# One written order for the spectrum products of a long-convolution kernel, and two weight loads on another queue

## The chip, the core and the metric

The kernel runs on one core of a Trainium2 chip. The time is device microseconds of one execution; the number given is the median of several runs. The core's engines are TensorE (PE), VectorE (DVE), ScalarE (ACT) and GpSimd (POOL); SyncE (SP), ScalarE and GpSimd issue DMAs. Each engine takes its instructions strictly in the order in which they stand in its program, and waits on semaphores for the others.

## What is computed

The reference runs two kinds of layer twice, forward, and then the gradients of all inputs. Layer A is a short convolution of `k` over four steps, a product with `v`, a convolution over the whole sequence by Fourier transform, and a gate; layer B is a dense network with SiLU.

```python
def _A_ref(q, k, v, shift_k, ssm_k, ssm_D):        # S = 2048, D = 448
    k_shift = sum(k_pad[:, t:t + S, :] * shift_k[:, ks - 1 - t] for t in range(ks))
    kv = k_shift * v
    y = irfft(rfft(kv padded to 2 S) * rfft(ssm_k padded to 2 S))[:S] + kv * ssm_D
    return q * y
x = A_q
x = x + _A_ref(_layernorm(x), A_k, A_v, ...); x = x + _B_ref(_layernorm(x), B_w1, B_w2)
x = x + _A_ref(_layernorm(x), A_k, A_v, ...); x = x + _B_ref(_layernorm(x), B_w1, B_w2)
```

`kv` and its convolution with `ssm_k` do not depend on `x`. They are made once, at the start, and used in both A layers.

## The kernel before

The function `_ssm_prefix` makes that convolution in the first 90 us or so. `Main` follows with both layers forward and backward, and `_ssm_suffix` with the gradients of the convolution. The change lies in the second half of `_ssm_prefix`, from `for i in range(4, 7)` (L499) to L560.

The transform has two stages. Stage 1 (`stage1_kv`, L465) writes the tile `A1kv`, and the same for the filter writes `KAB`. What follows works on 14 pieces of 1024 columns (numbered ci, 0 to 13), two of which make one block of 2048 (g, 0 to 6). For every piece or block there are these steps:

- **P and p** (`spec_k`, L468 to L475): the filter's stage 2. Two matmuls of 512 columns into a PSUM tile (`_fft_stage2_full`, L244), and a copy back to `KAB` by ScalarE (L116) or VectorE (L117). Pieces 0 to 7 are done between the convolutions; 8 to 13 in the loop at L499.
- **Q** (L474 and L282): GpSimd issues one store of two pieces to DRAM (`spec_K`) and four DMAs that write the other half of `KAB` with swapped partitions.
- **Z and z** (L511 to L516, the transposes at L514): 16 transposes of 128x128 of `A1kv` into one PSUM tile, and a copy to `ZkvA` or `ZkvB`. Block 3 lies across both and is copied in two halves.
- **F and f** (L244, and L523 or L116/L117): stage 2 of `kv`, two matmuls, and a copy back to `ZkvA` or `ZkvB`. After some pieces GpSimd issues a store to DRAM (`spec_KV`, L540).
- **M** (L542): VectorE multiplies piece ci with both halves of `KAB` into a tile `pab`, of which there are four.
- **V and v** (L253, L254): the inverse step, 16 matmuls from `pab` into PSUM, and a copy to `A1kv`, whose old contents are no longer needed.

All PSUM tiles of these steps share four slots of two banks (tag "A"). In the source the steps stand in loops: all p, then all Z, then for each ci F, f, M and, two pieces late, V. The order in which each engine then gets them is made by the compiler's scheduler, which ranks by place in the source and by an estimate of times, and so is the choice of PSUM slots. Which engine copies is chosen by `_Bal`, which adds up estimated times of ScalarE and VectorE and takes the lesser (L92 to L111).

The weights `w1` and `w2` of layer B are loaded in the same stretch. ScalarE issues the DMAs, behind its copies of pieces 4 and 7 (L523 to L534). First reader of `w1sb` is `Hh` (L638, L642), of `w2sb` it is `O` (L798).

After the stage come, on TensorE in a fixed order, the transposes of `grad_out` (L615) and `ys` (L563), which reads all of `A1kv`; ScalarE copies its results into `Ysb` (L564). VectorE makes the gate of the first chunk (L684, L685), which writes `X`, and its norm (L301 to L309), whose result is transposed (L626) for the first matmuls with `w1`. Four tile slots are used twice: `Ysb` lies where `ZkvA` was (tag W2), `X` where `ZkvB` was (WX), `w1sb` where `kT` was (W1), `w2sb` where `v_n` was (WB). A tile's first write waits until everything that read the earlier one is done, stores included.

Of the kernel before, what the change touches and what calls it, by code (L numbers as in the profile page):

```python
# [11 lines left out]
BF16 = mybir.dt.bfloat16  # L12
ACT = mybir.ActivationFunctionType
ALU = mybir.AluOpType
# [3 lines left out]
P = 128  # L18
S = 2048
D = 448  # L20
F = 1792
# [10 lines left out]
NCI = SPEC // 1024  # L32
# [81 lines left out]
def _copy(nc, eng, out, in_):  # L114
    if eng is nc.scalar:
        return nc.scalar.copy(out, in_)  # L116
    return eng.tensor_copy(out, in_)  # L117


KPARTS = [(0, 128), (128, 256), (256, 384), (384, 448)]  # L120


class K:
# [12 lines left out]
def kernel(  # L136
# [58 lines left out]
    k.mdp = ctx.enter_context(tc.tile_pool(name="mdp", bufs=1, reuse_waits="tile"))  # L195
    k.wtp = ctx.enter_context(tc.tile_pool(name="wtp", bufs=1, reuse_waits="tile"))
    ys = _ssm_prefix(k)
    k.psum = ctx.enter_context(tc.tile_pool(name="psum", bufs=1, space=PSUM, reuse_waits="tile"))
    k.bal.reset()
# [40 lines left out]
def _fft_stage2_full(k, Zf, ci, psum):  # L240
    ps = psum.tile([P, 1024], FP32, name="ps_s2", **k.pt["s2"])
    for hh in range(2):
        o = slice(hh * 512, hh * 512 + 512)
        k.nc.tensor.matmul(ps[:, o], lhsT=k.Gpre[:, G_FWDF, :] if ci % 2 else k.Gsb[:, G_FWD, :], rhs=Zf[:, o], start=True, stop=True)  # L244
    return ps


def _fft_inv_stage2_full(k, pa, pb, B1, ci, psum):
    nc = k.nc
    ga, gb = (G_IAF, G_IBF) if ci % 2 else (G_IA, G_IB)  # L250
    pv = psum.tile([P, 8, P], FP32, name="ps_v", **k.pt["v"])
    for i in range(8):
        nc.tensor.matmul(pv[:, i, :], lhsT=pa[:, i * P:(i + 1) * P], rhs=k.Gpre[:, ga, :], start=True, stop=False)  # L253
        nc.tensor.matmul(pv[:, i, :], lhsT=pb[:, i * P:(i + 1) * P], rhs=k.Gpre[:, gb, :], start=False, stop=True)  # L254
    _copy(nc, k.bal.pick(1024), B1[:, 8 * ci:8 * ci + 8, :].rearrange("p a b -> p (a b)"), pv[:].rearrange("p a b -> p (a b)"))


def _fft_inv_stage2_half(k, pa, pb, B1, ci, psum, cnd):
# [21 lines left out]
def _swap_halves_dma(k, dst, src, lo, hi):  # L280
    for o, i in SWAPS:
        k.nc.gpsimd.dma_start(out=dst[o, lo:hi], in_=src[i, lo:hi])  # L282


def _pm(ap2d):
    return ap2d.rearrange("(p j) d -> p j d", j=J)
# [47 lines left out]
def _ssm_prefix(k):  # L334
    nc, tc = k.nc, k.tc
    bal = k.bal
    k_pm = _pm(k.A_k[0])
    v_pm = _pm(k.A_v[0])
    with ExitStack() as es:
        spec = es.enter_context(tc.tile_pool(name="spec", bufs=1))  # L340
        work = es.enter_context(tc.tile_pool(name="pwork", bufs=2))
        psum = es.enter_context(tc.tile_pool(name="ppsum", bufs=3, space=PSUM))

        a_ = dict(tag="A", bufs=4)
# [4 lines left out]
        KAB = spec.tile([P, 2, SPEC], BF16, name="KAB")  # L349
        A1K = KAB[:, 0, :].rearrange("p (a c n s) -> p a c n s", c=2, n=16, s=2)  # L350
        A1Kf = KAB[:, 0, :].rearrange("p (a b) -> p a b", b=P)
        Ka = KAB[:, 1, :]
        Z = Ka.rearrange("p (a b) -> p a b", b=P)
# [15 lines left out]
        for h in range(2):  # L369
            for lo, hi in KPARTS[2 * h:2 * h + 2]:  # L370
                nc.sync.dma_start(out=ksb[lo // P][:hi - lo], in_=k.A_ssm_k[lo:hi, :])
# [14 lines left out]
        def k_turn(lo, hi):  # L386
            n = hi - lo
            kview = ksb[lo // P][:n].rearrange("p (n1 n2) -> p n2 n1", n2=16)
            pt = psum.tile([P, 2, 1024], BF16, name="ps_kt", **a_)
            pv = pt[:, :, 0:8 * n].rearrange("p g (i d) -> p g i d", d=n)  # L390
            for i in range(16):
                nc.tensor.transpose(pv[:, i // 8, i % 8, :], kview[:, i, :], k.ident[:n, :n])
            for g in range(2):
                _copy(nc, bal.pick(8 * n, dve_ns=0.53), Kt[:, 8 * g:8 * g + 8, lo:hi], pv[:, g])
# [12 lines left out]
        for lo, hi in ((0, 256), (256, D)):  # L407
            for plo, phi in KPARTS[lo // P:lo // P + 2]:
                k_turn(plo, phi)
# [17 lines left out]
        for jq in range(4):  # L427
            pt = psum.tile([DC, ND, 4, P], BF16, name="ps_kT", **a_)
# [40 lines left out]
        def spec_k(cp):  # L469
            for ci in (2 * cp, 2 * cp + 1):  # L470
                o = Ka[:, ci * 1024:(ci + 1) * 1024]
                _copy(nc, bal.pick(1024), o, _fft_stage2_full(k, o, ci, psum)[:])
            lo, hi = cp * 2048, (cp + 1) * 2048
            nc.gpsimd.dma_start(out=k.SPEC_d["K"][:, lo:hi], in_=Ka[:, lo:hi])  # L474
            _swap_halves_dma(k, KAB[:, 0, :], Ka, lo, hi)  # L475
# [20 lines left out]
        Zkv = [k.wk.tile([P, H2], BF16, name="ZkvA", tag="W2"), k.wk.tile([P, H2], BF16, name="ZkvB", tag="WX")]  # L496
        k.gb0 = _hd(k, [P, 4, D], "gb0")
        nc.sync.dma_start(out=k.gb0[:], in_=_pm(k.grad_out[0])[:, 0:4, :])
        for i in range(4, 7):  # L499
            spec_k(i)  # L500

        B1 = A1kv[:].rearrange("p b c n s -> p (b c n s)").rearrange("p (a x) -> p a x", x=P)

        def zkv(lo, hi):
            h = lo // H2
            return Zkv[h][:, lo - h * H2:hi - h * H2]

        def zdst(g):
            cuts = [(0, 16)] if g != 3 else [(0, 8), (8, 16)]
            return [(lo, hi, zkv(2048 * g + lo * P, 2048 * g + hi * P).rearrange("p (a b) -> p a b", b=P)) for lo, hi in cuts]  # L510
        for g in range(7):  # L511
            pt = psum.tile([P, 16, P], BF16, name="ps_tr", **a_)
            for i in range(16):
                nc.tensor.transpose(pt[:, i, :], B1[:, 16 * g + i, :], k.ident[:])  # L514
            for lo, hi, o in zdst(g):
                _copy(nc, bal.pick((hi - lo) * P, dve_ns=0.53), o, pt[:, lo:hi, :])  # L516
        hold = []

        def cons_prod(ci, ps):
            sl = slice(ci * 1024, (ci + 1) * 1024)  # L520
            xs = zkv(ci * 1024, (ci + 1) * 1024)
            if ci in (4, 7):
                with tc.issue_after(nc.scalar.copy(xs, ps[:]).ins):  # L523
                    if ci == 4:
                        w1x = k.wk.tile([P, ND * F + 2 * D], BF16, name="w1sb", tag="W1")
                        k.w1sb = w1x[:, 0:ND * F].rearrange("p (c f) -> p c f", f=F)
                        k.xq = [w1x[:, ND * F:].rearrange("p (j d) -> p j d", d=D)]
                        nc.scalar.dma_start(out=k.w1sb[:, 0:3, :], in_=k.B_w1[0:384, :].rearrange("(c p) f -> p c f", p=P))
                        nc.scalar.dma_start(out=k.w1sb[:, 3, :], in_=k.B_w1[320:448, :])
                    else:  # L530
                        w2x = k.wk.tile([P, (NF + 2) * D], BF16, name="w2sb", tag="WB")
                        k.w2sb = w2x[:, 0:NF * D].rearrange("p (c d) -> p c d", d=D)
                        k.xq.append(w2x[:, NF * D:].rearrange("p (j d) -> p j d", d=D))
                        nc.scalar.dma_start(out=k.w2sb, in_=k.B_w2.rearrange("(c p) d -> p c d", p=P))  # L534
                bal.add("act", 1.4)
            else:
                _copy(nc, bal.pick(1024), xs, ps[:])
            if ci in (1, 3, 5, 6, 8, 10, 12, 13):
                lo = (ci - (ci not in (6, 13))) * 1024
                nc.gpsimd.dma_start(out=k.SPEC_d["KV"][:, lo:(ci + 1) * 1024], in_=zkv(lo, (ci + 1) * 1024))  # L540
            pab = work.tile([P, 2, 1024], BF16, name="pab", tag="pab", bufs=4)
            nc.vector.tensor_tensor(out=pab[:], in0=xs.rearrange("p (o f) -> p o f", o=1).broadcast_to((P, 2, 1024)), in1=KAB[:, :, sl], op=ALU.mult)  # L542
            bal.add("dve", 1.25)
            hold.append((pab[:, 1], pab[:, 0], ci))
            if len(hold) > 2:
                pa, pb, cj = hold.pop(0)
                _fft_inv_stage2_full(k, pa, pb, B1, cj, psum)

        for ci in range(NCI):
            cons_prod(ci, _fft_stage2_full(k, zkv(ci * 1024, (ci + 1) * 1024), ci, psum))  # L550
        for pa, pb, cj in hold:
            _fft_inv_stage2_full(k, pa, pb, B1, cj, psum)

        B1v = B1.rearrange("p a (c n s) -> p a c n s", c=2, n=16)
        k.Ysb = k.wk.tile([P, J, D], BF16, name="Ysb", tag="W2")
# [819 lines left out]
```

## Time and profile before

| | us |
|---|---|
| median of 3 runs | 702.48 (701.94 to 702.93) |
| the profiled execution | 701.8 |
| its span in the profile | 700.0 |

The profile's page gives busy times of the engines over the span, a picture in 40 slices, the chain of work that ended last, groups of instructions by source line, and DMA issues. Other answers of the trace give the same for a window, in order of time (timeline), or as sums of who waited for whom. In a timeline a row is: start, duration, engine, line, operation, written tile, read tiles, shapes, count; in square brackets the idle time of that engine before it and what ended it. PE is TensorE, DVE VectorE, ACT ScalarE, POOL GpSimd. A duration is longer than the distance from one start to the next, since instructions of one engine overlap a little.

### The profile page before, as it was taken

Reading aid. Unit: us, or ns where it says so; the run is one execution under the profiler, and the core shown is the slowest. Engines: PE = TensorE matmul, PEld = TensorE weight load, DVE = VectorE, ACT = ScalarE, POOL = GpSimd, SP = SyncE. Lnnn points to the kernel's source line nnn. Section 1 sums busy time; section 2 is a strip of 40 time slices with the busy share of each in tenths; the row PEclk is TensorE's granted clock in tenths of the full one; section 3 lists DMA queues with packets and bytes.
Section 4 is the critical chain, followed back from the end, with each engine's and each line's share of the span. In section 5 each row is a group of like instructions: output and inputs, shape, how many; then the busy total and the mean of one; then the engine's idle time right before and its main releaser. Section 6 shows DMA issues by size and latency. Waiting matters only on the chain.

```text
span 700.0 us, 14553 instructions
## 1 busy us (share of the span) xinstructions
PE 666.0 (95%) x5897; PEld 358.8 (51%) x5933; DVE 484.1 (69%) x1131; ACT 432.9 (62%) x522; POOL 101.3 (14%) x173
## 2 busy tenths in 40 slices
PE   6898789999999999999999999999999999999996
PEld 5876545454444444434444444544554555555664
DVE  6688862676889948899578874853946545538991
ACT  5888766968856857769577585223554553554431
POOL 1057110110011100111000100010111211102311
PEclk9999999999999999999999999999999999999999
DMA  8999938459899976698677799959557888966981
GB/s 321 270 298 306 376 84 210 118 107 243 219 231 249 246 200 166 146 240 221 185 165 194 194 242 329 262 172 229 177 208 280 307 279 307 352 188 215 331 293 42
DMA packets 199798, 161.03 MB, mean 230 GB/s; under 512 B 147698, under 2 KB 180213, under 8 KB 198963
## 3 DMA queue, kind: packets, MB, share of 16 engines
q1 hardware_dynamic: 184550, 111.78, 58.8%
q0 software_dynamic: 10368, 36.29, 15.3%
q10 hardware_dynamic: 4812, 12.04, 5.0%
q8 instruction: 46, 0.75, 0.4%
q14 instruction: 22, 0.17, 0.1%
HBM read 66.05 MB, written 54.60 MB: 172 GB/s over the span
## 4 chain that ended last, share of the span: by engine, by line
PE 57%; DVE 22%; issue 10%; ACT 5%; POOL 3%; DMA 2%; POOLq 0%; DVEq 0%; ACTq 0%
PE ps_d L1046 19%; PE ps_n L836 8%; PE ps_h L638 6%; PE ps_g L638 6%; PE ps_o L798 5%; DVE ln_st L301 2%; DVE lb_v L994 2%; PE ps_v L265 2%; PE ps_cv L449 2%; POOL rstd L306 2%; DVE n L309 1%; DVE lb_v L997 1%; DVE lb_v L998 1%; DVE X L802 1%; PE ps_h L642 1%
## 5 line engine op out<-in xcount | busy, mean ns | idle before, releaser
L1046 PEld LDWEIGHTS <-dstat 128*128 128x128 bf16 x896 | 84.0, 98 | 77.8 <-issue 4.0
L836 PE MATMUL ps_n<-w1T,ghT 128*128 128x448 bf16 x448 | 96.6, 353 | 2.0 <-DVE ghT L821 1.7
L798 PE MATMUL ps_o<-w2sb,aT 128*128 128x448 bf16 x448 | 89.2, 353 | 0.7 <-DVE X L802 0.7
L638 PE MATMUL ps_h<-nT,w1sb 128*128 128x512 bf16 (+1 forms) x410 | 83.5, 336 | 2.2 <-ACT Dall L116 1.0
L116 ACT CAST ghT<-ps_g 128x1024 bf16<-128x1024 f32 (+1 forms) x54 | 48.4, 899 | 58.4 <-PE ps_g L642 47.7
L638 PE MATMUL ps_g<-nT,w2T 128*128 128x512 bf16 x317 | 77.9, 379 | 2.2 <-DVE Dall L117 0.5
L836 PEld LDWEIGHTS <-ghT 128*128 128x128 bf16 x448 | 41.4, 98 | 50.7 <-DVE ghT L821 6.7
L798 PEld LDWEIGHTS <-aT 128*128 128x128 bf16 x448 | 43.2, 98 | 41.1 <-issue 2.8
L638 PEld LDWEIGHTS <-w1sb 128*128 128x128 bf16 x420 | 39.2, 98 | 36.7 <-issue 7.2
L781 ACT ACTIVATE aT<-ps_h 128x1024 bf16<-128x1024 f32 (+1 forms) x48 | 44.2, 921 | 19.4 <-PE ps_h L638 10.5
L116 ACT CAST Dall<-ps_h 128x1024 bf16<-128x1024 f32 (+2 forms) x60 | 54.3, 904 | 0.0
L994 DVE SCALAR_TENSOR_TENSOR lb_v<-lb_u,n 128x448 bf16<-128x448 bf16 x60 | 37.2, 620 | 24.6 <-ACT lb_u L840 24.1
L791 ACT ACTIVATE Dall<-Dall 128x1024 bf16<-128x1024 bf16 (+1 forms) x48 | 53.2, 1186 | 0.1
L638 PEld LDWEIGHTS <-w2T 128*128 128x128 bf16 x336 | 31.3, 98 | 42.1 <-issue 7.2
L306 POOL TENSOR_TENSOR rstd<-ln_ve,mhalf 128x2 f32<-128x2 f32 (+1 forms) x24 | 19.9, 831 | 221.1 <-DVE ln_ve L305 221.1
L1046 PE MATMUL ps_d<-X,dstat 128*128 128x448 bf16 x224 | 47.9, 353 | 0.0
L1046 PE MATMUL ps_d<-go,dstat 128*128 128x448 bf16 x224 | 47.2, 353 | 0.0
L1046 PE MATMUL ps_d<-n3m,dstat 128*128 128x448 bf16 x224 | 46.4, 353 | 0.0
L1046 PE MATMUL ps_d<-n1m,dstat 128*128 128x448 bf16 x224 | 46.3, 353 | 0.0
L840 ACT ACTIVATE lb_u<-ps_n,rstd 128x448 bf16<-128x448 f32 x32 | 20.5, 640 | 28.7 <-PE ps_n L836 24.3
L116 ACT CAST A1g<-ps_v 128x1024 bf16<-128x1024 f32 x14 | 14.9, 1066 | 36.5 <-PE ps_v L265 36.5
L802 DVE TENSOR_TENSOR X<-X,ps_o 128x448 bf16<-128x448 bf16 x32 | 19.5, 610 | 21.3 <-PE ps_o L798 21.1
(206 smaller groups left out, 1111.6 us busy)
## 6 DMA issues: line engine op xcount, KB each, us to landing
dstat<-a_d SPq DMA_DIRECT2D x28, 512.0 KB, 5.0
dstat<-g_d SPq DMA_DIRECT2D x28, 512.0 KB, 5.2
a_d<-turned SPq DMA_DIRECT2D x16, 512.0 KB, 3.0
g_d<-turned SPq DMA_DIRECT2D x16, 512.0 KB, 3.2
a_d<-turned SPq DMA_DIRECT2D x16, 384.0 KB, 2.7
g_d<-turned SPq DMA_DIRECT2D x16, 384.0 KB, 3.0
spec_K<-KAB POOLq DMA_DIRECT2D x7, 512.0 KB, 5.4
KAB<-KAB POOLq DMA_DIRECT2D x28, 128.0 KB, 4.6
```

What stands on the lines that cost most here:

```text
L116: return nc.scalar.copy(out, in_)
L265: nc.tensor.matmul(pv[:, r ^ (ci & 1), i, :], lhsT=src[ri, i * P:(i + 1) * P], rhs=k.Gsb[ri, g, ri], start=first, stop=not first)
L306: nc.gpsimd.tensor_tensor(out=r[:, lo:hi], in0=ve[:, lo:hi], in1=k.mhalf[:, lo:hi], op=ALU.pow)
L638: self.nc.tensor.matmul(ps, lhsT=w[:, b, ft * P:(ft + 1) * P], rhs=x[:, b], start=(start and b == 0), stop=(stop and b == bs[2]))
L781: self.last_silu = nc.scalar.activation(aT[hh][:, o:o + hi - lo, :], ps(lo, hi), ACT.Silu)
L791: self.nc.scalar.activation(dT[hh][:, o:o + n, :], dT[hh][:, o:o + n, :], ACT.Derivative_silu)
L798: nc.tensor.matmul(po[:, :D], lhsT=aT[ft // 7][:, ft % 7, tl * P:(tl + 1) * P], rhs=self.w2sb[:, ft, :], start=(ft == 0), stop=(ft == NF - 1))
L802: self.last_o = nc.vector.tensor_tensor(out=X[:, t, :], in0=X[:, t, :], in1=po[:, :D], op=ALU.add)
L836: nc.tensor.matmul(pn[:, :D], lhsT=gh[ft // 7][:, ft % 7, tl * P:(tl + 1) * P], rhs=self.w1T[:, ft, :], start=(ft == 0), stop=(ft == NF - 1))
L840: nc.scalar.activation(u0[:], pn[:, :D], ACT.Identity, scale=k.rstd[2 * L + 1][:, t:t + 1], accum_out=cp[:, tl, 0:1])
L994: nc.vector.scalar_tensor_tensor(out=v[:], in0=u0, scalar=-1.0 / D, in1=n_t, op0=ALU.mult, op1=ALU.mult, accum_out=cp[:, 1:2])
L1046: self.nc.tensor.matmul(ps[:, :D], lhsT=st[:, t, :], rhs=mov[:, t, :], start=(first and t == 0), stop=(last and t == NT - 1))
```

## The change

The steps of the stage from P8 on are written as one list of tokens. A capital is work on TensorE (P, Z, F, V), on VectorE (M) or the DMAs of a Q; a small letter is the copy out of PSUM, with its engine as the last letter, `a` for ScalarE and `d` for VectorE (`z3y` and `z3x` are the two halves of block 3). The list is traced in a `manual_schedule` of TensorE, ScalarE, VectorE and GpSimd: each of these engines gets its instructions of the list in the list's order.

```diff
+PRODUCTS = """
+P9 P10 P11 P12 p9a p10d p11a P13 p12d P8 p8a Z0 Q5 p13d Z1 z0d Z2 z1a Q6 F0 z2d F1 f0a F2 f1d F3 f2a F4 Q4 M0 F5 f3a Z4
+f4a Z6 z4d f5a z6d F8 f8a F9 M1 F12 F13 f9a Z5 M2 f12a V0 z5d f13a Z3 v0a F11 z3yd z3xd F7 f11a M3 F6 f7a F10 V1 M4 f6a
+V2 f10a M6 V3 v1a M5 V4 v2a M11 V5 v3a V6 M10 v4a V11 M12 v5a V10 M13 v6a V12 v11a M7 V13 v10a M8 V7 v12a M9 V8 v13a v8d
+V9 v7a v9a
+"""
...
-        for i in range(4, 7):
-            spec_k(i)
...
-                _copy(nc, bal.pick((hi - lo) * P, dve_ns=0.53), o, pt[:, lo:hi, :])
...
-                        nc.scalar.dma_start(out=k.w1sb[:, 0:3, :], in_=k.B_w1[0:384, :].rearrange("(c p) f -> p c f", p=P))
-                        nc.scalar.dma_start(out=k.w1sb[:, 3, :], in_=k.B_w1[320:448, :])
...
+            seen.add(ci)
+            for lo, hi in ((0, 2), (2, 4), (4, 6), (6, 7), (7, 9), (9, 11), (11, 13), (13, 14)):
+                if ci in range(lo, hi) and seen >= set(range(lo, hi)):
+                    nc.gpsimd.dma_start(out=k.SPEC_d["KV"][:, lo * 1024:hi * 1024], in_=zkv(lo * 1024, hi * 1024))
+                    if lo == 6:
...
+                        nc.gpsimd.dma_start(out=k.w1sb[:, 0:3, :], in_=k.B_w1[0:384, :].rearrange("(c p) f -> p c f", p=P))
+                        nc.gpsimd.dma_start(out=k.w1sb[:, 3, :], in_=k.B_w1[320:448, :])
+                    elif lo == 9:
...
+                        nc.gpsimd.dma_start(out=k.w2sb, in_=k.B_w2.rearrange("(c p) d -> p c d", p=P))
...
+        do = dict(P=P_, p=p, Q=Q, Z=Z_, z=z, F=F_, f=f, M=M, V=V, v=v)
+        with tc.manual_schedule(engines={e.engine for e in (nc.tensor, nc.scalar, nc.vector, nc.gpsimd)}):
+            for tok in PRODUCTS.split():
+                args = [int("".join(x for x in tok if x.isdigit()))]
+                if tok[-1] in "ad":
+                    args += [int(tok[-2] == "y"), nc.scalar if tok[-1] == "a" else nc.vector]
+                do[tok[0]](*args)
```

The stores of `spec_KV` keep their eight ranges of pieces; each is issued when its last piece has been copied, so their order follows the list: (0,1), (2,3), (4,5), (13), (11,12), (7,8), (6), (9,10). The loads of `w1` come right behind the store of piece 6 and that of `w2` right behind the store of pieces 9 and 10, all on GpSimd's queue. The matmuls, products and copies are the same in number and shape as before.

## The prediction

> **What bounds the kernel now.** I read the page first. TensorE fills 95% of the span, and the chain that ended last is TensorE work for 57% of it, so the kernel is one long dependent chain. A stage that ends earlier moves everything behind it, unless a transfer stops that. The change touches one stage only, from the last convolution work to `ps_y`, 52.5 to 90.7 us. So I asked for busy times in that stretch (columns: length, PE, weight loads, VectorE, ScalarE, GpSimd, clock, DMA share, GB/s).
>
> ```profile
> PE 666.0 (95%) x5897; PEld 358.8 (51%) x5933; DVE 484.1 (69%) x1131; ACT 432.9 (62%) x522; POOL 101.3 (14%) x173
> ...
> 52.50:90.70 38.20, 29.59 (x405) 22.70 (x407) 32.48 (x30) 29.59 (x30) 15.96 (x32) 1.00 0.96 329
> ```
>
> No engine is full: in 38.2 us TensorE has 29.6, VectorE 32.5, ScalarE 29.6. The DMA engines are full (0.96). So the stage is bound either by the order of the work on in-order engines, or by transfers. The waits of 52 to 91 us tell which (engine, tile and line, what it waited for: us in total, times, longest):
>
> ```profile
> PE ps_v L253 <- DVE pab L542: 7.4, 7, 2.4
> ACT A1kv L116 <- PE ps_v L254: 4.5, 4, 2.4
> DVE ZkvB L117 <- PE ps_s L244: 1.8, 1, 1.8
> DVE A1kv L117 <- PE ps_v L254: 1.3, 2, 1.2
> ```
>
> All are engines waiting for each other, none for a transfer. The timelines show one such wait:
>
> ```profile
> 77.37 2.35 DVE L542 TENSOR_TENSOR pab<-ZkvB,KAB 128x2048 bf16<-128x2048 bf16 x2
> 81.50 1.23 DVE L117 CAST ZkvB<-ps_s 128x1024 bf16<-128x1024 f32 x1 [1.78 <-PE ps_s L244]
> 82.64 3.48 DVE L542 TENSOR_TENSOR pab<-ZkvB,KAB 128x2048 bf16<-128x2048 bf16 x3
> ...
> 78.39 1.02 ACT L116 CAST ZkvB<-ps_s 128x1024 bf16<-128x1024 f32 x1
> ...
> 80.87 0.59 PE L244 MATMUL ps_s<-ZkvB,Gsb 128*128 128x512 bf16 x2
> 83.91 0.23 PE L253 MATMUL ps_v<-Gpre,pab 128*128 128x128 bf16 x1 [2.45 <-DVE pab L542]
> ```
>
> ScalarE had piece 10 ready at 79.4. But VectorE's queue holds the cast of piece 12 ahead of product 10, and that cast needs a matmul that starts at 80.87. VectorE stands for 1.78, then TensorE for 2.45. That is a wrong order, not a lack of engine time. The chain leaves the stage by the last cast:
>
> ```profile
> 89.36 1.24 DVE A1kv L117
> 90.60 0.14 issue
> 90.73 0.93 PE ps_y L563 x4
> 91.69 0.92 ACT Ysb L564
> ```
>
> **Terms.** Pitches (start to start) from the timelines: ScalarE cast of 1024, 0.91 (three from 62.54 take 2.84); ScalarE turn copy of 2048, 1.79; VectorE cast, turn copy and product, each 1.14 (three products from 63.58 take 3.50); half a turn copy 0.60; forward pair F or P on TensorE 0.43; seven turns in 6.41, 0.90 each; an inverse V of 16 matmuls 0.90. The profiled execution took 701.8 (span 700.0); the runs' median is 702.48, 0.7 more. The sums below are differences inside the profiled one, and I take them off the median.
>
> **Work.** Same operations, other engines. ScalarE before: 27 casts and 2 turn copies, 28.2; after: 29 and 1, 28.2. VectorE before: 7 casts, 4 turn copies and 2 halves, 14 products, 29.7; after: 5, 5 and 2, 14, 28.6. TensorE is 27.5 in both. So 1.1 us less on VectorE; the rest must come from waits.
>
> **The walk.** I went through the written list token by token with these pitches: each operation starts when its engine, its inputs and one of the four PSUM slots are free, 0.06 us after its releaser. The start is that of before: TensorE at 52.5, ScalarE 52.85, VectorE 54.40 (its last `A1kv` cast, 53.40 to 54.47). VectorE comes out as the one that binds:
> - It goes through p10, p12, p13, z0, z2, f1, M0 with 0.08 of waiting.
> - z4 waits 0.56 for its turn; z3 waits 0.50 for its turn at 68.1.
> - From M3 at 70.4 it runs eleven products without a gap, and M9 starts at 81.8.
> - 54.40 + 27.4 (28.56 without the last cast v8) + 1.1 of waits = 83.0. Then V9 1.06, cast v9 on ScalarE 1.02, hand-overs: **85.2**.
>
> In the same manner the order of before comes out at 91.0, where the trace has 90.6: the walk is 0.4 long, and it finds the 1.8 wait above. So the stage ends 5.4 us earlier (5.8 by the walk against itself). Where waits go: before, VectorE alone stood 5.7 in seven gaps of 0.17 to 1.78. What is late next is the product chain itself. A row may be off by 0.02 us on 28 operations, 0.5 in all.
>
> **Swaps (Q).** Products need swapped halves that GpSimd issues: a store of 0.54 and four swaps of 0.49. The list puts Q5, Q6, then the store of F0 and F1, then Q4. In the trace the three sets issue between 57.2 and 67.3 and the last lands at 72.4. With that store ahead, Q4 lands about 74.1 and M8 runs at 80.7; Q5 lands about 65 and M11 runs at 75.0. Cost nothing, cover 6 us or more; beyond it, one for one.
>
> **w1 and w2.** ScalarE loses three issues, which cost it no gap in the timeline. GpSimd gains three, after f6 (72.6 in the walk) and f10 (73.5). No such load is in the trace on that queue; its issues run from 0.49 to 0.96. GpSimd has nothing behind them but the last store and then the norm's `rstd`, at 95.8 before, so the issues cost nothing. Landing: before, 11.9 and 13.6 us (w1) and 17.0 (w2). w1 is first read at 102.3, moved to 96.9, and w2 ten us after it: room of some 9 us.
>
> **The last store.** This is the dear one. On GpSimd's queue the store of pieces 9 and 10 now goes behind w1. `X` takes the slot of `ZkvB` (tag WX), so VectorE's first write of `X`, 93.29 before and 87.9 after, must wait for that store. The rows:
>
> ```profile
> 68.00:72.00 4.00, 2.77 (x39) 2.00 (x38) 4.00 (x4) 4.00 (x5) 1.07 (x2) 1.00 0.99 272
> 76.00:80.00 4.00, 2.97 (x36) 2.17 (x38) 3.72 (x4) 2.58 (x4) 0.60 (x2) 1.00 1.03 406
> ...
> spec_KV<-ZkvB POOLq DMA_DIRECT2D x3, 512.0 KB, 7.7
> spec_KV<-ZkvB POOLq DMA_DIRECT2D x1, 256.0 KB, 3.5
> ```
>
> The DMA engines are full through both, at 272 GB/s with stores nearly alone and at 406 mixed with the weights. The last store (issued 87.24) landed at 90.8, 2.5 ahead of `X`. After: Q4 at 74.1; five half-megabyte units of stores at 1.7 (307 GB/s, the queue alone from 50 to 68) 82.6; w1, 1.84 MB at 390 GB/s (386 to 406 from 76 to 88), 87.3; the store, 89.0. Ends: 86.9, if all the bytes end at 90.8 as before and only w2 (1.6 MB, 3.9) lies behind; 93.2, if each store takes 2.3, as the first one did behind the last swap. I take 89.0, by the row of the same queue. Behind `X` come norms and the transpose of `n` at 98.18, 0.6 after its input: slack 0.6. Hold = 89.0 - 87.9 - 0.6 = 0.5, between 0 and 4.7. `Ysb` takes `ZkvA`'s slot in the same way: needed at 86.3, stores landed 82.6 to 86.2.
>
> The trace shows both queues moving side by side from 72 to 88, 3.2 MB on ScalarE's and 3.0 on GpSimd's, while GpSimd's transfers landed in their issue order. The Trainium skill ("DMA: Bandwidth & Descriptors", Queues, rings and completion order) says that each DMA engine goes round-robin between the queues that have work, and takes one queue's ring in order. By that rule the store is certain to wait for the whole of w1 (the hold of 0.5, by that estimate); without it the store could overtake, and the hold would be 0.
>
> Behind the stage nothing stands at a fixed time: `ys`, the `w1T` load and the rest follow `ps_y`. **Sum:** 5.4 - 0.5 = 4.9; 702.5 - 4.9 = **697.6**.
>
> **Rivals.**
> - *Forecast*: the order works, hold 0 to 2.5: 697.1 to 699.6. 0.66.
> - *Better*: the walk's 0.4 bias and VectorE's 1.1 of waits go too: 695.5 to 697. For it: VectorE bound. Against: turns must be made first. 0.08.
> - *Stores slow*: 2.3 each, hold 2.5 to 4.7: 699.6 to 701.8. For it the 272 row; against it 307. 0.13, of it 0.04 within 0.2%.
> - *Nothing*: the list binds the engines but not the PSUM slots, which are given out by a time estimate; V's then wait for the wrong slot as often as VectorE waited before: 702.5. Against: four slots, and both walks need few waits on them. 0.05.
> - *Slower*: GpSimd's queue moves w1 badly, and `X` waits for it. Nearest row: `Minvs`, 1 MB on that queue, 8.4 us to landing; w1 at that rate takes 14.6 instead of 4.7, the store lands at 98.9, hold 10.4: 707.5. It turns the sign from a landing at 93.9 on. For it: nothing that large ran on this queue here; against: `Minvs` shared the engines with other loads. 0.08.
>
> A measurement here can tell about 0.2% (1.4 us) from no change. Faster 0.66 + 0.08 + 0.09 = 0.83, within 0.04 + 0.05 = 0.09, slower 0.08. Range 695.5 to 701.0: all of forecast and better, and the faster part of slow stores, 0.83.
>
> **What would show it.** Right: last `A1kv` cast on ScalarE ending near 85; VectorE without a gap over 0.6 after 54.4; eleven products in a row; `ps_y` near 85.4; a wait of `X` for a `spec_KV` transfer of 0 to 3. Wrong: products waiting for `KAB` swaps, `ps_h` waiting for w1, `Ysb` waiting for `spec_KV`, or a stage that ends at 85 and a span that doesn't move.

## The result and the profile after

The changed kernel takes **698.35 us** (median of 7 runs, 697.08 to 700.83) beside 702.93 (701.85 to 703.41, 7 runs) for the kernel before: ratio 0.9937, 95% interval [0.9925, 0.9948]. The profiled execution took 698.35, with a span of 696.5 (before: 701.8 and 700.0).

A span is the sum of four distances on TensorE: to the first P matmul behind the last stage 1 matmul (the start), from there to the first `ps_y` (the stage), on to the first `ps_h` (the matmuls with `w1`), and to the end.

| | before | after | difference |
|---|---|---|---|
| start | 52.53 | 53.39 | +0.86 |
| stage | 38.21 | 32.51 | -5.70 |
| `ps_y` to `ps_h` | 11.53 | 12.34 | +0.81 |
| `ps_h` to the end | 597.75 | 598.28 | +0.53 |
| span | 700.01 | 696.51 | -3.50 |

The stage gained what the walk had promised. The start is 0.86 later in this execution; ahead of it every engine has the same instructions in the same order, and over all executions below it moves between 52.46 and 55.04. It is no part of the change. The 0.81 is the wait for the last store, as `store_first` below shows.

The busy times of the changed kernel between its first P and its first `ps_y` (same columns as before):

```profile
53.39:85.90 32.51, 30.39 (x410) 23.25 (x409) 31.16 (x29) 29.39 (x31) 18.74 (x35) 1.00 0.99 324
```

VectorE is busy for 31.2 of 32.5 us, where before it was 32.5 of 38.2. The waits of 53 to 90 us, in the same form as before:

```profile
DVE X L710 <- DMA spec_KV<-ZkvB: 1.4, 1, 1.4
...
ACT Ysb L589 <- DMA spec_KV<-ZkvB: 1.1, 1, 1.1
...
ACT A1kv L116 <- PE ps_v L261: 0.6, 1, 0.6
```

The 7.4 of TensorE waiting for products is gone, and of the 4.5 of ScalarE waiting for the inverse steps 0.6 is left. The largest left on VectorE is one for a transfer. The row of `Ysb` also names a store, and `Ysb` waiting for `spec_KV` was one of the prediction's signs of being wrong. It is no such wait: in `store_first` below the same idle time before `Ysb`, 1.05, is put down to `ps_y`, and here too `Ysb` starts 1.00 after the first `ps_y`, as there. VectorE's timeline shows the product chain and its end:

```profile
63.76 2.35 DVE L117 COPY ZkvB<-ps_tr 128x2048 bf16<-128x2048 bf16 x2 [0.44 <-PE ps_tr L531]
...
69.91 0.69 DVE L117 COPY ZkvB<-ps_tr 128x1024 bf16<-128x1024 bf16 x1 [0.39 <-PE ps_tr L531]
70.51 0.68 DVE L117 COPY ZkvA<-ps_tr 128x1024 bf16<-128x1024 bf16 x1
71.11 4.62 DVE L561 TENSOR_TENSOR pab<-ZkvA,KAB 128x2048 bf16<-128x2048 bf16 x4
75.65 8.03 DVE L561 TENSOR_TENSOR pab<-ZkvB,KAB 128x2048 bf16<-128x2048 bf16 x7
83.70 1.23 DVE L117 CAST A1kv<-ps_v 128x1024 bf16<-128x1024 f32 x1
...
89.89 0.63 DVE L710 TENSOR_TENSOR X<-x0c,a_t 128x896 bf16<-128x896 bf16 x1 [1.42 <-DMA spec_KV<-ZkvB]
```

Two waits of 0.44 and 0.39 for turns, then eleven products with nothing between them. At 89.89 `X` starts 1.42 after VectorE was free, for the last store. TensorE stands 0.45 for it, and the transposes of `n` behind that take 0.87, where they take 0.62 in the kernel before:

```profile
93.91 0.87 PE L651 MATMUL ps_t<-ident,n 128*128 128x128 bf16 x8 [0.45 <-DVE n L316]
```

From the trace's DMA records: `w1` landed at 87.29 and 88.39, the store of pieces 9 and 10 (issued 77.15) at 89.67, `w2` at 94.14: in the order of issue.

### The profile page after: what moved, and what is told of

Its sections match the earlier page's. It is cut to its first block, busy times and chain, and to the rows that moved or that the text cites. A ratio compares the mean times of both kernels' runs of the same rounds, so it can differ in the third digit from the quotient of the medians.

```text
span 696.5 us, 14591 instructions
## 1 busy us (share of the span) xinstructions
PE 671.3 (96%) x5933; PEld 361.1 (52%) x5933; DVE 482.4 (69%) x1130; ACT 432.6 (62%) x523; POOL 103.8 (15%) x176
## 4 chain that ended last, share of the span: by engine, by line
PE 54%; DVE 20%; issue 11%; DMA 6%; POOL 4%; ACT 4%; POOLq 0%; ACTq 0%; DVEq 0%
PE ps_d L1071 19%; PE ps_n L861 8%; PE ps_h L663 6%; PE ps_g L663 6%; PE ps_o L823 5%; DVE ln_st L308 3%; PE ps_v L272 2%; DVE lb_v L1019 2%; DMA spec_K<-KAB 2%; POOL rstd L313 2%; DMA spec_KV<-ZkvB 2%; DVE n L316 1%; DVE X L827 1%; PE ps_h L667 1%; DVE lb_v L1023 1%
## 5 line engine op out<-in xcount | busy, mean ns | idle before, releaser
L663 PE MATMUL ps_g<-nT,w2T 128*128 128x512 bf16 x336 | 79.5, 379 | 1.0 <-DVE Dall L117 0.5
```

Of the source, the lines that this page charges most:

```text
L663: self.nc.tensor.matmul(ps, lhsT=w[:, b, ft * P:(ft + 1) * P], rhs=x[:, b], start=(start and b == 0), stop=(stop and b == bs[2]))
```

## Experiments

**Theory:** the order of the list, with its copying engines, shortens the stage by 5.7; the new queue for the weights gains nothing, and costs a wait of `X` for the last store. **Rivals:** the queue is the gain; any fixed order would do; the order alone does it, whatever engine copies; VectorE's 1.1 less work does it.

All runs, with medians and ranges, the ratio to the kernel before on the same chip, and three numbers from each profile:

| run | us | ratio, 95% interval | stage | `ps_y` to `ps_h` | wait of `X` |
|---|---|---|---|---|---|
| before | 702.93 | 1 | 38.21 | 11.53 | 0 |
| the change | 698.35 (697.08 to 700.83) | 0.9937 [0.9925, 0.9948] | 32.51 | 12.34 | 1.42 |
| after_again | 697.76 (696.73 to 704.25) | 0.994 [0.9921, 0.9959] | 32.51 | 13.80 | 2.88 |
| store_first | 697.16 (696.94 to 697.98) | 0.9918 [0.9904, 0.9932] | 32.50 | 11.58 | 0 |
| store_first_2 | 697.68 (697.3 to 698.03) | 0.9919 [0.9906, 0.9932] | 32.49 | 11.57 | 0 |
| weights_ahead | 704.82 (702.6 to 707.85) | 1.0024 [1.0011, 1.0038] | 32.50 | 19.13 | 5.94 |
| weights_scalar | 701.71 (699.67 to 705.93) | 0.999 [0.9972, 1.0009] | 37.77 | 12.94 | 0 |
| weights_scalar_late | 699.38 (697.36 to 705.84) | 0.9961 [0.9939, 0.9983] | 34.34 | 11.60 | 0 |
| queue_only | 706.13 (704.58 to 706.98) | 1.0037 [1.0023, 1.0052] | 39.86 | 11.53 | 0 |
| old_order | 704.29 (702.47 to 710.7) | 1.0029 [1.0007, 1.005] | 38.58 | 12.20 | 1.33 |
| old_picks | 702.75 (702.24 to 705.35) | 0.9999 [0.9986, 1.0012] | 37.92 | 11.57 | 0 |
| walked | 696.9 (695.57 to 699.1) | 0.9913 [0.99, 0.9927] | 31.51 | 11.53 | 0 |

### The change once more

> The changed kernel once more, on the chip of the three that follow. Both theories: 698.4, between 697 and 701; stage from the first P matmul to ps_y 32.5; X waits 1.4 for the last spec_KV store, and TensorE 0.45 at the transpose of n.

The stage came out at 32.51 again, to the hundredth, from a start of 52.48. The wait of `X` did not: 2.88, since the last store landed at 90.21 although the stage ended 0.9 earlier than in the first profile. The store did not come earlier with the engines.

### The weights behind or ahead of the last store

`store_first` puts `w1` behind the last store, `weights_ahead` puts `w2` ahead of it as well:

```diff
-                    if lo == 6:
+                    if lo == 9:
...
-                    elif lo == 9:
```

That is `store_first`; `weights_ahead` takes out the second branch alone, so that `w2` follows `w1` behind piece 6:

```diff
                     if lo == 6:
...
-                    elif lo == 9:
```

> The two w1 loads are issued behind the store of pieces 9 and 10 instead of ahead of it; nothing else differs. Theory (X is held by the last store because w1 lies ahead of it in the same queue, slack 0.6 to 1): the store lands 4 to 5 earlier, near 85, X follows a_t without a wait, TensorE's 0.45 at the transpose of n goes; 697.9, 0.5 below the changed kernel. w1 lands near 89, its reader comes at 98. Rival (the store is late by the DMA engines' total load, not by its place in the queue): it lands near 89.7 again and X waits 1.4.

> w1 and w2 both ahead of the store of pieces 9 and 10 on GpSimd's queue. Theory (hold grows one for one beyond the slack): the store lands 4 to 4.5 later, near 94, X waits 5.5 to 6, time 4 above the changed kernel: 702.5. Rival (work between X and the first matmul with w1 has room to absorb it): less than 2 above.

VectorE of `store_first`:

```profile
87.19 0.62 DVE L708 TENSOR_TENSOR a_t<-na,Ysb 128x896 bf16<-128x896 bf16 x1 [1.14 <-ACT Ysb L588]
87.84 0.63 DVE L709 TENSOR_TENSOR X<-x0c,a_t 128x896 bf16<-128x896 bf16 x1
```

`X` follows `a_t` at once: the store, issued at 73.76, landed at 82.73, five us ahead of `X` (near 85 was expected). `w1` landed at 87.08 and 88.19, as in the changed kernel, so nothing is lost by its place. (GpSimd issued `w2` only at 91.35, behind a `rstd`; why is not shown. It landed at 99.83 and nothing waited for it.) From `ps_y` to `ps_h` the time is 11.58, within 0.05 of before: the 0.81 and the 2.27 of the two profiles of the change were this wait.

`weights_ahead` cost more than the wait alone: 704.82, where 702.5 was expected. VectorE and TensorE, and TensorE's granted clock in one window (the column behind GpSimd's):

```profile
93.50 0.63 DVE L709 TENSOR_TENSOR X<-x0c,a_t 128x896 bf16<-128x896 bf16 x1 [5.94 <-DMA spec_KV<-ZkvB]
```

```profile
97.53 1.23 PE L650 MATMUL ps_t<-ident,n 128*128 128x128 bf16 x8 [4.97 <-DVE n L316]
98.55 3.19 PE L587 MATMUL ps_y<-A1kv,Minvsb 128*128 128x448 bf16 x8
```

```profile
96.00:100.00 4.00, 2.46 (x12) 1.42 (x13) 3.81 (x10) 0.00 (x0) 1.02 (x2) 0.56 0.00 0
```

The store landed at 93.28, 1.23 behind `w2` (92.05): one queue, in the order of issue. `X` waited 5.94, TensorE stood 4.97, to 97.53, and its granted clock was 0.5 for 6.83 us, from 96.47 on. So from `ps_y` to `ps_h` it took 19.13, 7.6 more than with no wait: 5.0 of standing, and 2.6 in the work behind it, most of which ran at half clock. (The eight `ps_y` took 3.19, as against 1.68 in `store_first`.) It cancels the whole gain of the stage.

### The weights on ScalarE's queue, with the new list

`weights_scalar` keeps the list and issues `w1` and `w2` from ScalarE where the kernel before does, behind the copies of pieces 4 and 7. `weights_scalar_late` issues them from ScalarE behind pieces 6 and 10, where the change has them on GpSimd. The edit of the first (the second has 6 and 10 for 4 and 7; the branches on GpSimd are taken out in both):

```diff
+            if ci == 4:
...
+                    nc.scalar.dma_start(out=k.w1sb[:, 0:3, :], in_=k.B_w1[0:384, :].rearrange("(c p) f -> p c f", p=P))
+                    nc.scalar.dma_start(out=k.w1sb[:, 3, :], in_=k.B_w1[320:448, :])
+            elif ci == 7:
...
+                    nc.scalar.dma_start(out=k.w2sb, in_=k.B_w2.rearrange("(c p) d -> p c d", p=P))
```

> The written order, but w1 and w2 issued by ScalarE behind its copies of pieces 4 and 7 as before the change. Theory (stores and weights share the DMA engines, so weights on another queue take half the engines from the stores and swaps): the last stores land at 90 to 92, X waits 2 to 4, the first Ysb copy is held up to 3 by the stores of ZkvA, ps_y itself stays within 1 of the changed kernel; 699.5 to 702. Rival (the order is the whole gain, and the queue only adds the hold of X): no wait at X, 697.9.

> The changed kernel's order, with w1 and w2 issued by ScalarE behind the copies of pieces 6 and 10, that is at the change's places in the list, on the other queue. Theory (the loss of the early places on ScalarE was the early start, which slowed the swaps): no product waits for KAB, 32.5 us from the first P to ps_y, the last store lands at 88 to 90, X waits 0 to 2; 697.5 to 699.5. Rival (weights on ScalarE's queue cost some 4 us wherever they are issued): 701.5.

The first missed on the stage: it was 37.77, not 32.5, and nearly the whole gain was gone. That its time, 701.71, lies in what was expected (699.5 to 702) is luck in part, for `X` had no wait and only `Ysb` was held. VectorE and TensorE of `weights_scalar`:

```profile
84.29 2.36 DVE L561 TENSOR_TENSOR pab<-ZkvB,KAB 128x2048 bf16<-128x2048 bf16 x2 [3.24 <-DMA KAB<-KAB]
```

```profile
85.58 0.29 PE L260 MATMUL ps_v<-Gpre,pab 128*128 128x128 bf16 x1 [3.40 <-DVE pab L561]
```

The new list reaches these copies early: `w1` is issued at 62.01, while GpSimd's swaps are under way. A set of four swaps that landed 3.8 to 4.5 us after its issue in the changed kernel now took 9.8 to 10.7, GpSimd issued the next ones later, and the last of Q4 landed at 84.17 in place of 75.27. Product 8 waited for it. The stores came late in turn, and `Ysb` waited 3.0 for one from `ZkvA`, which is the 12.94 in the table. So the place of the loads, and with it the queue, is a condition for the gain, though no source of it.

The late run's time, 699.38, is just inside what the theory expected (697.5 to 699.5), but by another path. No product waited for swaps and `X` had no wait, but the stage was 34.34, 1.8 too long, for a reason that neither expected. ScalarE's own timeline (ACTq is its issue of DMAs):

```profile
72.48 2.11 ACTq L547 DMA_DIRECT2D w1sb<-in_B_w_dram  x1
74.63 1.01 ACT L116 CAST ZkvB<-ps_s 128x1024 bf16<-128x1024 f32 x1 [1.36 <-PE ps_v L261]
74.73 1.88 ACTq L552 DMA_DIRECT2D w2sb<-in_B_w_dram  x1
76.65 5.59 ACT L116 CAST A1kv<-ps_v 128x1024 bf16<-128x1024 f32 x6 [1.01 <-issue]
```

Two issues took 2.11 and 1.88, and ScalarE stood 1.36 and 1.01 around them, each time with casts queued that TensorE and then VectorE's next product waited for. In the changed kernel GpSimd issues the same loads in 0.78, 0.57 and 1.11, with nothing urgent behind them. The time is 1.6 above that of `after_again`.

### The queue alone

`queue_only` is the kernel before, with `w1` and `w2` issued on GpSimd behind the stores of piece 6 and of pieces 9 and 10; the order is left to the scheduler.

> The kernel before, with w1 moved to GpSimd's queue behind the store of piece 6 and w2 behind that of pieces 9 and 10; the order of the stage is left to the scheduler as it was. Theory (the written order is the gain, the queue alone gives nothing): first P to ps_y 38 us, the last store lands near 91 and X, at 93.3, does not wait; 702.3 to 703.6. Rival (the queue is the gain, since the written order with the weights on ScalarE's queue came out at 701.7): 698 to 700.

No gain, so the rival falls; but 706.13 is also 2.5 above the theory. The scheduler ranked this source differently: VectorE's first cast of an inverse step now stands a product earlier and waits for a matmul:

```profile
76.44 1.23 DVE L117 CAST A1kv<-ps_v 128x1024 bf16<-128x1024 f32 x1 [1.35 <-PE ps_v L254]
```

The stage is 39.86, 1.65 longer than before, by an edit that moved three DMA issues. The rest of the profile's excess is a start of 55.04: the granted clock was 0.5 for 6.83 us from 29.2 on, ahead of anything that was changed. Not every execution of it has that: one with a mean granted clock of 0.999 (the profiled one has 0.993) took 705.87 all the same. So what the median has beyond the 1.65 is open.

### The old order, and the old copying engines, written out

`old_order` replaces the list by the order and engines that the trace of before shows (from P8 on; the weights stay on GpSimd). `old_picks` keeps the new list and gives each copy to the engine that made it before:

```diff
-P9 P10 P11 P12 p9a p10d p11a P13 p12d P8 p8a Z0 Q5 p13d Z1 z0d Z2 z1a Q6 F0 z2d F1 f0a F2 f1d F3 f2a ...
+P9 P10 P11 P12 p9a p10d p11a P13 p12a P8 p8a Z0 Q5 p13d Z1 z0d Z2 z1d Q6 F0 z2a F1 f0a F2 f1a F3 f2a ...
```

> The changed kernel with another list: the order and the copying engines that the trace of the kernel before shows, written out as tokens; the weights stay on GpSimd's queue. Theory (what counts is which order it is): the walk gives 38.5 us from the first P to ps_y; 702.5 to 703.5. Rival (that the order is fixed at all, with its choice of PSUM slots, is the gain): below 700.

> The changed kernel's list, with the copying engines of the kernel before (7 casts, 4 turn copies and 2 halves on VectorE). Theory (VectorE binds, and copies handed to the wrong engine make ScalarE and VectorE wait for each other): the walk gives 38.2 us from the first P to ps_y, with a wait of 3.4 us at v8; 702.5 to 703.5. Rival (the order of the tokens carries it, the engines add only the 1.1 us more work on VectorE): 699.5.

The walk gave 38.5 and 38.2 for the stage; measured were 38.58 and 37.92. `old_order` brings the wait of 1.78 back on VectorE, and 2.45 on TensorE with it (its time, 704.29, is 0.8 above what was expected; `X` waits 1.33 in it too):

```profile
81.72 1.22 DVE L117 CAST ZkvB<-ps_s 128x1024 bf16<-128x1024 f32 x1 [1.78 <-PE ps_s L248]
```

```profile
84.13 0.23 PE L257 MATMUL ps_v<-Gpre,pab 128*128 128x128 bf16 x1 [2.45 <-DVE pab L558]
```

In `old_picks` the waits sit elsewhere. VectorE waits for a copy that ScalarE has behind others, and at the end ScalarE waits for the inverse step of piece 8, whose product VectorE makes late:

```profile
63.37 1.22 DVE L558 TENSOR_TENSOR pab<-ZkvA,KAB 128x2048 bf16<-128x2048 bf16 x1 [2.24 <-ACT ZkvA L116]
```

```profile
89.60 2.85 ACT L116 CAST A1kv<-ps_v 128x1024 bf16<-128x1024 f32 x3 [3.25 <-PE ps_v L258]
```

The walk had 3.4 for the last wait. So neither a fixed order, nor this order without its engines, gains anything; VectorE's 1.1 less work explains at most a fifth of the 5.4 that the engines make. The old order with the new engines was not run.

### A list searched for with the walk

`walked` has `store_first`'s loads and another list, found by moving tokens and changing copying engines until the walk's last cast came at 83.35 (85.24 for the change's list). It begins:

```
P12 p12a P9 P10 p10d Z0 P11 p9a P13 p11a p13a Z1 z0d Q5 P8 p8a Q6 Z2 F0 z1d F1 f0a z2d Z4 f1a z4d F3 F2 Q4 F4 F8 f2d
```

> The list replaced by one searched for with the walk of the prediction (moves of tokens and other copying engines, the walk's last cast as the measure), and w1 and w2 behind the last store as in the earlier run. The walk gives a last cast 1.9 us earlier than for the changed kernel's list (83.35 against 85.24). Theory (the stage is the sum of rows along in-order engines, which the walk adds up): 30.6 us from the first P to ps_y, no wait of X; 1.9 less than the run with w1 behind the store, 695.3. Rival (the walk leaves out what a list tuned otherwise meets, such as the swaps' landing or the stores' turn on GpSimd, and the gain is eaten by waits for transfers): 32 to 33 us, 697 to 698.

> The run with w1 behind the last store once more, beside the searched list on the same chip: 697.2, within 0.6.

The stage is 31.51, 1.0 shorter than `store_first`'s and not 1.9. Both numbers missed: no transfer is waited for, so the rival's reason falls, but the walk promised twice what came. VectorE:

```profile
67.33 1.22 DVE L117 COPY ZkvB<-ps_tr 128x2048 bf16<-128x2048 bf16 x1 [0.35 <-PE ps_tr L531]
...
71.06 2.36 DVE L560 TENSOR_TENSOR pab<-ZkvA,KAB 128x2048 bf16<-128x2048 bf16 x2 [0.23 <-PE ps_v L261]
73.33 8.03 DVE L560 TENSOR_TENSOR pab<-ZkvB,KAB 128x2048 bf16<-128x2048 bf16 x7
```

These two waits, of 0.35 and 0.23, are for turns and for an inverse step. What the walk has in their place is not on record, so where the 0.9 was lost is open. It may be that a list chosen because the walk likes it uses the walk's errors as well; that is argued and not shown. Its median is the lowest of all, but its interval overlaps that of `store_first`.

## Why the prediction was right, point by point

- **What binds:** right. In the changed kernel VectorE waits for another engine only twice between the start and its last cast of the stage, 0.44 and 0.39, and `old_order` brings back the 1.78 and the 2.45 together with the old stage.
- **Work (VectorE 1.1 less):** right as a count, and rightly not taken as the gain: `old_picks` gives the 1.1 back and loses 5.4.
- **The walk (5.4, 5.8 against itself):** right. 5.70 measured, and four more executions of this list have the same stage within 0.02; the two waits for turns, said to be 0.56 and 0.50, were 0.44 and 0.39, and the eleven products came in a row.
- **Swaps at nothing:** right. The last landed at 75.27, 1.2 later than said, or 0.3 measured from the stage's start; no product waited. What the point lacked: it named 6 us of cover against an early store, and not that loads beside the swaps can eat it, as `weights_scalar` did.
- **Weights' issue at nothing:** right on GpSimd. That ScalarE lost nothing when its issues left was taken from the old timeline; in the new list they would have cost 1.8 (`weights_scalar_late`).
- **The last store (0.5, between 0 and 4.7):** the right mechanism, too small a size. The path from `ps_y` to `ps_h` grew by 0.81 and by 2.27, each 0.6 less than the wait of `X` (1.42 and 2.88), which is the slack that was said. Landing was said to be 89.0 and was 89.67 and 90.21. The term that was off is the rate of `w1`: the five half-megabyte units of stores were to be done at 82.6 and were (82.03 with a later start), but `w1` landed 6.4 and 7.2 us behind them, where 4.7 was reckoned from the rate of two queues together. The store behind it came sooner than the 1.7 that was said, after 1.28. The upper end of the landing, 93.2, is also added wrongly: with 2.3 for each store and 4.7 for `w1` it is 92.6, a hold of 4.1. The rule that the prediction cited from the Trainium skill ("DMA: Bandwidth & Descriptors", Queues, rings and completion order) agrees with what these runs show: the store landed 1.28 behind `w1` here and 1.23 behind `w2` in `weights_ahead`, never ahead of what was issued before it; and loads on ScalarE's queue slowed the swaps of GpSimd's to 10.7, as turns between two queues would.
- **Nothing behind the stage stands at a fixed time:** right up to `ps_h`. From there to the end every other profile has 598.1 to 599.5, where the one of before has 597.75. What makes these 0.4 or more is open; the one profile of before may be the short one.
- **Sum:** 4.9 said, 4.6 measured (702.93 to 698.35). The stage gave 0.3 more than said and the store took 0.3 to 1.8 more; that the two nearly cancel in the first profile is luck. The rival of slow stores (a hold of 2.5 to 4.7) is nearly what the second profile of the change shows. Of the rival in which inverse steps wait for the wrong slot nothing showed: no matmul of `ps_v` is in the list of waits. Of the slower rival the mechanism was right and the price low: it let the sign turn from a landing at 93.9 on, and `weights_ahead` is 1.9 slower than the kernel before with a landing at 93.3, because standing can cost clock as well.

## What to carry to other kernels

On in-order engines a stage in which none is full is worth walking by hand, with the durations of one trace: here the walk came within 0.4 us of a stage of 32 to 39 for three lists, and within 1 for one that was searched with it. Order and choice of engine belong together; half of a good schedule gave nothing. Whatever a tile's slot waits for, a store to DRAM above all, goes ahead of loads that nobody needs yet: moving `w1` behind the last store took away the one wait that the change had added.

## What the runs showed of the hardware

A stall of TensorE can cost more than its length. In `weights_ahead` TensorE stood from 92.56 to 97.53, and the granted clock was 0.5 for 6.83 us from 96.47 on; in `weights_scalar` it stood 3.40, to 85.58, and the clock was 0.5 for 3.41 us from 85.54 on. The Trainium skill ("TensorE: Matmul & The Clock Gate", Part 1: The HAM clock gate) says that an idle window of about 3.4 us, in a frame that runs freely, halves the clock; the lengths agree with that. The threshold does not: the wait of 2.45 in `old_order`, from 81.68 to 84.13, was followed by 3.41 us at 0.5 from 85.06 on, while one of 2.45 at the same place in the kernel before was not. The 3.41 us ahead of 85.06 hold that whole wait and 0.93 of work. TensorE's windows of `old_order` and, behind it, of before:

```profile
84.00:88.00 4.00, 3.87 (x39) 3.33 (x40) 3.14 (x4) 2.13 (x3) 0.55 (x2) 0.63 1.01 403
```

```profile
84.00:88.00 4.00, 3.25 (x50) 2.79 (x50) 3.15 (x3) 2.98 (x4) 0.54 (x1) 1.00 1.03 386
```

So a stall of two to three us costs clock in one execution and not in another. The mean granted clock of the other executions points the same way. Of the 19 executions of the change, the four above 700 us (700.42 to 704.25) have 0.994 to 0.996 and the fifteen others 0.996 to 0.999; the nine of `store_first` and `store_first_2` have 0.996 to 0.999 and lie between 696.94 and 698.03. Where the longer executions lost their clock is not shown, since the trace keeps one execution of each run. It need not be in this stage: the profile of `store_first_2` has 3.41 us at 0.5 from 31.58 on.
